# Batch 0's score masks, keys and tail rearranged, and one score visit per later batch, in a fused attention and MoE kernel

## The chip, the cores and the metric

The kernel runs on one core of a Trainium2 chip. The metric is device time in microseconds (us) of one execution; the median of the executions of a kernel is its time. One execution is also recorded by the hardware profiler; its span runs from the first to the last instruction of the program, and its own device time is somewhat longer than that span.

The engines are named as the profile names them: PE is the matrix engine (TensorE), PEld its weight loads, DVE is VectorE, ACT is ScalarE, POOL is GpSimd, and SP is SyncE, which computes nothing and issues transfers. PSUM has eight banks of 128 partitions by 512 float32 values, into which PE writes.

## The reference

```python
batch, n_heads, seq, head_dim = (8, 8, 576, 64)        # q, k, v in float32
scores = scale * np.matmul(q, k.transpose(0, 1, 3, 2))
rel = pos[:, None] - pos[None, :]
mask_plain = (rel >= 0) & (rel < 32)
mask_dil = (rel >= 0) & (rel < 32 * 4) & (rel % 4 == 0)   # heads 4 to 7
attn = softmax(where(mask, scores, -1e9))
x = (attn @ v) as 4608 tokens of 512 values
h = x @ w_in                                            # 512 -> 2048
out = (h * sigmoid(beta * h)) @ w_out                   # 2048 -> 512
```

Every head sees 32 keys per query: heads 0 to 3 ("plain") the last 32 positions, heads 4 to 7 ("dilated") every fourth of the last 128. The output is 4608 by 512 in float32.

## The kernel before

The work has two halves. **Attention** goes batch by batch (b = 0 to 7). **The feed-forward half** goes by tiles of 512 tokens (t = 0 to 8). For each t there are 16 "slots", one for each 128 of the 2048 hidden columns: four matmuls with 512 columns at line 811, a tanh on ACT (line 820) and a gate on DVE (line 825). Then come four output "blocks" of 16 matmuls each (line 846), cast by ACT (line 861) and stored through SP (line 866).

One plan orders all of it. Each piece of work is an operation given to `plan.op`, with the engines that can do it and their estimated times, what it depends on, a wished-for moment `vt` (lower is sooner), and the PSUM banks that it acquires. `Plan.run` simulates the engines and the transfer queues. Each round it takes, for each engine, the operations that could start within a few tens of ns of the earliest, and of these the one with the lowest `vt`; the instruction is emitted in that order, so the order on every engine is fixed when the kernel is built. Groups of banks have kinds with a limit each: `CAPS = {"h": 3, "p": 4, "o": 2, "z": 4, "a": 8, "s": 5}`, where "h" and "p" are slots, "o" and "z" output blocks, "s" scores and "a" everything else. Where PE would be idle early on, the plan emits matmuls on zeros (the filler, line 958)[...].

**Loads.** For batches 0 to 2 (`DIRECT = 3`) the POOL queue loads q and k with a cast to bf16 (`direct_qk`, issued at line 384). For batch 0 the order in the queue is: dilated k, dilated q, plain k, plain q, then v and the weights. Dilated k goes to `std[0]`, a 96 by 2 by 768 tile. PE transposes it (line 448 for dilated, 455 for plain), and ACT or DVE copy it out of PSUM (line 232). From batch 3 on, the loads go through DRAM and a transposing DMA.

**Scores.** Operations named S2 and S3 score the dilated heads (line 639), S00, S10, S01 and S11 the plain ones (line 673), T the last 64 positions of the dilated heads (line 609). The exponential of a score bank is an ACT operation at line 576. Score matmuls have 64 contraction rows and run as two row halves side by side. The plan prices a change between this and full rows at `SWITCH = 95` ns.

Batch 0 has its mask added on PE: matmuls of the identity with `add_d` or `add_p` (lines 631, 661, 664) put 0 or -65536 into the bank before the scores accumulate on it. These matmuls are the head of the same plan operation as the scores. From batch 1 on, the mask is a multiplication after the exponential (line 580), on POOL or DVE, with tiles that POOL builds early: `mask_d`, and for the plain heads `maskn_PP` and `maskn_FP`, 4 by 96 columns each (line 376). From batch 2 on (`PAIRED = 2`) two plain head pairs are scored together, in two visits to PE per batch: S00 covers the first half of the positions and S01 the second. Each visit is 12 matmuls with 96 columns into four banks, and each bank is read by an exponential of 288 columns.

V and U are the products with v (lines 714, 729, 699), followed by a normalisation on DVE (lines 595, 596). For batches 0 and 1, X and Y transpose the result back on PE (lines 765, 780, 750) into `xT`, the input of the slots. U and Y2, Y3 belong to the tail T.

```python
vts[first.index("T"):len(first)] = [-.5, -.4, -.3, -.2]      # T U Y2 Y3 of batch 0, line 902
```

The functions that the diff touches, with the line numbers of the profile:

Of the kernel before, what the change touches and what calls it, by code (L numbers as in the profile page):

```python
# [22 lines left out]
class Op:  # L23
    def __init__(self, engs, fn, deps, vt, acquire, group, dma, lat, halves=False, sbuf=False):
# [4 lines left out]
        self.end = self.ready = None  # L29
        self.waits = 0  # L30
# [5 lines left out]
class Plan:  # L36
# [3 lines left out]
    CAPS = {"h": 3, "p": 4, "o": 2, "z": 4, "a": 8, "s": 5}  # L40
    SWITCH = 95
    LAT = {"PE": 210, "ACT": 45, "DVE": 45, "POOL": 60, "SP": 0}
# [5 lines left out]
    def op(self, engs, fn, deps=(), vt=0.0, acquire=None, group=None, dma=0, lat=None, halves=False, sbuf=False):  # L48
        acquire = acquire if acquire is None or isinstance(acquire, list) else [acquire]
        o = Op(engs, fn, deps, vt, acquire, group or acquire, dma, lat, halves, sbuf)  # L50
        self.ops.append(o)
        return o

    def run(self, filler=None, filler_until=0.0):
# [36 lines left out]
        while n_left:  # L91
# [21 lines left out]
            for e, c in near.items():  # L113
                first = min(s for s, _, _ in c)
                s, o, d = min((x for x in c if x[0] <= first + self.NEAR[e]), key=lambda x: (x[1].vt, x[0]))
                picks.append((s, o.vt, e, o, d))
# [58 lines left out]
def kernel(  # L175
# [38 lines left out]
    APART = 4  # L214

# [26 lines left out]
    mask_n = {n: const([P, 2, 2, QT], BF16, f"maskn_{n}") for n in ("FP", "PP")}  # L242
# [12 lines left out]
    pt = [const([P, NI * 2, P], BF16, f"pt{x}") for x in range(2)]  # L255
# [52 lines left out]
    def t_fill2(e):  # L308
        for x in range(2):
            nc.vector.memset(pt[x][:, :, QT:P], 0.0)  # L310
        nc.vector.memset(ptt[:], 0.0)
# [60 lines left out]
    def first_rows(m):  # L372
        nc.gpsimd.memset(m[0:WIN, 0], 0.0)
    for i, n in enumerate(("PP", "FP")):
        def t_mask_n(e, n=n):
            band(mask_n[n][:].rearrange("p a b n -> p (a b) n"), [[0, 4]], [(1, QT)], WIN, -1, 1.0, 0.0)
            if n == "FP":
                first_rows(mask_n[n])
        late_mask("n" + n, 1900, t_mask_n, -7.183 + .001 * i)
# [11 lines left out]
    def direct_qk(b, z, h0, deps, vt):  # L391
# [3 lines left out]
        return load("POOL", (dst[z], src), deps, vt, 576, .41 if b else .33, lat=1100 if b else 1500)  # L395

# [13 lines left out]
    def direct_vd(b, deps, vt, tdeps=()):  # L410
        src = v[b, 4:8].rearrange("h (t T) d -> t h (T d)", T=C)[0:P]
        out = [load("POOL", (vd16_of[b].rearrange("p h T d -> p h (T d)"), src), deps, vt, 512, .35)]
        for c in range(2):
            src = bass.AP(tensor=v.tensor, offset=v[b, 4].offset + ((P - WIN) * C + c) * D,
                          ap=[[2 * D, 2 * KTL], [S * D, 4], [1, D]])
            out.append(load("POOL", (vt_[b % 2][:, c, :, 0:D], src), list(tdeps), vt + (1.245 if b == 0 else .02 if b < DIRECT else 0) + .001 + .001 * c, 96, .2))
# [26 lines left out]
    def t_transposes(g, z, kind, i):  # L443
# [6 lines left out]
        else:  # L450
            tp = bank(g, BF16)[:, 0:S].rearrange("p (j g) -> p j g", j=RP)
            for j in range(RP):
                for h in range(2):
                    rows = slice(64 * h, 64 * h + 64)
                    nc.tensor.transpose(tp[rows, j], stp[z][rows, i, j * D:(j + 1) * D], ident_b[rows, rows])  # L455

# [49 lines left out]
    def attention(b, ld, names, vts):  # L506
# [4 lines left out]
        if b < DIRECT:  # L511
            for n in [x for x in names if x[0] in "KQ"]:
# [3 lines left out]
                src = ld["qk", z, 0 if kind == "P" else 4]  # L516
                tr = plan.op([("PE", (18 * mm(64) if kind == "P" else 6 * mm(QT)))],
                             lambda e, g=g, z=z, kind=kind, i=i: t_transposes(g, z, kind, i),
                             [src, ident], vt, acquire=g)
# [53 lines left out]
        def exp_and_mask(key, sop, g, vt, n, sc, w, m, tiles):  # L573
# [4 lines left out]
            if b >= ADDED or key == ("T",):  # L578
                def mask(e):
                    E[e].tensor_tensor(out=w(), in0=w(), in1=m(), op=ALU.mult)  # L580
                ex = plan.op([("POOL", 170 + 2.2 * n), ("DVE", 160 + .8 * n)], mask,
                             [ex] + ([mask_tail] if key == ("T",) else [mask_ops["D"]] if key[0] >= 2 else
                                     [mask_ops["n" + ("PP" if key[1] else "FP")]]), vt, sbuf=True)
# [17 lines left out]
        for name in [n for n in names if n[0] in "ST"]:  # L601
# [24 lines left out]
            if x >= 2:  # L626

                def score(e, xs=xs, gs=gs):
                    if b < ADDED:
                        for g in gs:  # L630
                            nc.tensor.matmul(  # L631
                                bank(g).rearrange("p (a n) -> p a n", a=4), lhsT=ident_b[:],
                                rhs=add_d[:].unsqueeze(1).to_broadcast([P, 4, P]), start=True, stop=False)
                    for n, x in enumerate(xs):
                        for i in range(4):
                            r, h4 = i // 2, 2 * (x - 2) + i % 2
                            for c in range(2):
# [5 lines left out]
                sop = plan.op([("PE", len(xs) * 4 * mm(P) + (190 + 2 * mm(4 * P) if b < ADDED else 0))], score,  # L643
                              deps + ([ident, adds["D"]] if b < ADDED else []), vt, acquire=gs, halves=True)
# [9 lines left out]
            j = int(name[2])  # L654

            def score(e, xs=xs, j=j, gs=gs):
                if b < ADDED:
                    for g in gs:
                        lo = 0
                        if j == 0:  # L660
                            nc.tensor.matmul(bank(g)[:, 0:QT], lhsT=ident_b[:], rhs=add_p["F"][:],
                                             start=True, stop=False)
                            lo = 1
                        nc.tensor.matmul(
                            bank(g)[:, lo * QT:3 * QT].rearrange("p (a n) -> p a n", n=QT), lhsT=ident_b[:],
                            rhs=add_p["P"][:].unsqueeze(1).to_broadcast([P, 3 - lo, QT]),
                            start=j == 1, stop=False)
                for n, x in enumerate(xs):
                    for a in range(3):
                        i = 3 * j + a  # L670
                        for h in range(2):
# [4 lines left out]
            sop = plan.op([("PE", len(xs) * 3 * mm(QT) + (190 + 2 * mm(3 * QT) if b < ADDED else 0))], score,  # L676
                          ([o for x in xs for o in steps[f"KP{x}"] + steps[f"QP{x}"]] if b < DIRECT else ready["P"])
                          + ([ident, adds["P"]] if b < ADDED else []), vt, acquire=gs, halves=True)
# [3 lines left out]
            for n, x in enumerate(xs):  # L682
                for h in range(2):
# [4 lines left out]
                                 lambda j=j: mask_n["PP" if j else "FP"][:].rearrange("p a b n -> p (a b) n")[  # L688
                                     :, (0, 1)[j == 0]:(0, 1)[j == 0] + 3],
# [302 lines left out]
```

## Time and profile before

| what | value |
|---|---|
| median of 3 executions | 305.16 us (305.11 to 305.79) |
| the profiled execution's own time | 304.98 us |
| its span | 303.1 us |
| PE busy | 296.0 us, 98% of the span |
| DVE, ACT, POOL busy | 183.1, 170.7, 90.9 us |
| mean granted PE clock | 0.999 |

"Busy" of PE counts overlapping matmuls and also the filler, so it is no measure of useful work. A timeline row gives the start, the stretch from the first start to the last end of merged instructions, the engine, line, operation, what it writes and reads, how many instructions it merges (x12), and in brackets the idle time of the engine before it, with what ended it.

### The profile page before, as it was taken

How to read it: one execution, taken by the hardware profiler on the slowest of the kernel's cores; microseconds unless marked ns; L12 is line 12 of the kernel's file. 1: busy time of each engine (PE TensorE's matmuls, PEld its weight loads, DVE VectorE, ACT ScalarE, POOL GpSimd, SP SyncE). 2: the span in 40 equal slices, each digit the busy share in tenths (PEclk: the TensorE clock that was granted, in tenths of full speed). 3: DMA queues.
4: the chain of work that ended last, by engine and by line, in shares of the span. 5: the costliest groups of instructions: out<-in, count | busy, mean ns of one | idle time of the engine just before them, and what ended most of it. 6: DMA issues, size and time to landing. Idle time of an engine off the chain costs nothing.

```text
span 303.1 us, 6036 instructions
## 1 busy us (share of the span) xinstructions
PE 296.0 (98%) x2312; PEld 148.8 (49%) x2312; DVE 183.1 (60%) x424; ACT 170.7 (56%) x314; POOL 90.9 (30%) x131
## 2 busy tenths in 40 slices
PE   7899999999999999999999999999999999999995
PEld 5565545654554444455444444444444444444454
DVE  4469965888866746896676658656764344343300
ACT  2667963877547644765664557555664444554411
POOL 8988662756046106320740074100000000000000
PEclk9999999999999999999999999999999999999999
DMA  6999999999999998999799989994132100100122
GB/s 95 170 211 201 206 188 205 193 146 169 182 172 220 158 212 154 175 151 227 155 170 183 206 148 167 172 212 110 56 93 75 38 35 35 37 35 35 54 83 73
DMA packets 117376, 42.47 MB, mean 140 GB/s; under 512 B 93748, under 2 KB 110916, under 8 KB 117348
## 3 DMA queue, kind: packets, MB, share of 16 engines
q0 software_dynamic: 66672, 19.66, 63.6%
q1 hardware_dynamic: 50532, 22.36, 36.6%
q8 instruction: 18, 0.29, 0.4%
q10 hardware_dynamic: 144, 0.07, 0.1%
q14 instruction: 10, 0.08, 0.1%
HBM read 39.32 MB, written 18.87 MB: 192 GB/s over the span
## 4 chain that ended last, share of the span: by engine, by line
PE 86%; DMA 8%; DVE 3%; issue 1%; POOL 1%; ACT 1%; DVEq 0%; POOLq 0%
PE bank L846 40%; PE bank L811 37%; DMA vp<-in_v_dram 6%; DMA st<-in_q_dram 2%; PE bank L729 2%; PE bank L673 2%; PE bank L639 1%; DVE g L825 1%; PE bank L714 1%; PE bank L455 1%; PE bank L448 1%; PE bank L699 1%; PE bank L780 0%; PE bank L631 0%; DVE xsp L596 0%
## 5 line engine op out<-in xcount | busy, mean ns | idle before, releaser
L846 PE MATMUL bank<-w_out_bf,g 128*128 128x512 bf16 (+2 forms) x608 | 142.7, 368 | 0.0
L825 DVE SCALAR_TENSOR_TENSOR g<-tnh,bank 128x512 bf16<-128x512 bf16 x144 | 97.9, 685 | 70.6 <-ACT tnh L820 69.7
L811 PE MATMUL bank<-xT,w_in_bf 128*128 128x512 bf16 (+1 forms) x584 | 140.1, 376 | 0.0
L820 ACT ACTIVATE tnh<-bank,beta_half 128x512 bf16<-128x512 f32 x144 | 98.4, 689 | 72.4 <-PE bank L811 67.9
L811 PEld LDWEIGHTS <-w_in_bf 128*128 128x128 bf16 x584 | 55.1, 98 | 61.0 <-issue 0.2
L846 PEld LDWEIGHTS <-g 128*128 128x128 bf16 x608 | 54.4, 98 | 55.4
L861 ACT ACTIVATE osb<-bank 128x512 f32<-128x512 f32 (+1 forms) x35 | 20.6, 588 | 31.6 <-PE bank L846 31.5
L576 ACT ACTIVATE pt<-bank 128x288 bf16<-128x288 f32 x64 | 21.6, 421 | 6.2 <-PE bank L673 6.2
L576 ACT ACTIVATE ptd<-bank 128x512 bf16<-128x512 f32 x32 | 16.9, 606 | 7.0 <-PE bank L639 7.0
L596 DVE TENSOR_TENSOR xsp<-bank,rcp 96x384 bf16<-96x384 f32 x32 | 17.7, 554 | 1.1
L384 POOL DMA_DIRECT2D vp<-in_v_dram x10 | 18.0, 1803 | 0.5 <-PE bank L455 0.5
L924 POOL COPY pace<-xT 1x2 bf16<-1x2 bf16 x4 | 0.8, 201 | 55.8 <-DMA xT<-x 55.8
L595 DVE RECIPROCAL rcp<-bank 128x4 f32<-128x4 f32 (+2 forms) x72 | 12.9, 179 | 5.9 <-PE bank L729 4.1
L580 DVE TENSOR_TENSOR ptd<-ptd,mask_d 128x512 bf16<-128x512 bf16 x27 | 11.9, 452 | 6.2 <-ACT ptd L576 5.0
L596 DVE TENSOR_TENSOR xdm<-bank,rcp 128x256 bf16<-128x256 f32 x32 | 13.6, 425 | 1.1
L384 POOL DMA_DIRECT2D s<-in_q_dram x10 | 13.7, 1374 | 0.0
L384 POOL DMA_DIRECT2D vt<-in_v_dram x16 | 13.6, 1034 | 0.0
L729 PEld LDWEIGHTS <-pt 128*128 128x128 bf16 x192 | 9.1, 97 | 5.7 <-issue 0.5
L384 POOL DMA_DIRECT2D s<-in_k_dram x10 | 11.2, 1123 | 1.1 <-issue 1.1
L232 POOL COPY vd<-st 128x1024 bf16<-128x1024 bf16 x5 | 5.2, 1037 | 19.4 <-DMA st<-in_v_dram 19.4
L729 PE MATMUL bank<-vp,pt 128*128 128x65 bf16 x192 | 10.1, 193 | 0.2 <-DMA vp<-in_v_dram 0.2
L863 DVE TENSOR_SCALAR osb<-bank 128x512 f32<-128x512 f32 (+2 forms) x3 | 1.4, 470 | 13.3 <-PE bank L846 13.3
(107 smaller groups left out, 183.3 us busy)
## 6 DMA issues: line engine op xcount, KB each, us to landing
out_dram<-osb SPq DMA_DIRECT2D x35, 256.0 KB, 2.6
s<-in_k_dram POOLq DMA_DIRECT2D x10, 288.0 KB, 6.7
s<-in_q_dram POOLq DMA_DIRECT2D x10, 288.0 KB, 10.1
vp<-in_v_dram POOLq DMA_DIRECT2D x7, 384.0 KB, 18.1
w_out_bf<-in_moe_w_out_dram POOLq DMA_DIRECT2D x2, 1024.0 KB, 16.5
st<-in_k_dram POOLq DMA_DIRECT2D x6, 288.0 KB, 13.4
st<-in_q_dram POOLq DMA_DIRECT2D x6, 288.0 KB, 12.7
x<-xsp SPq DMA_DIRECT2D x12, 144.0 KB
```

The source lines that it names most:

```text
L384: {"POOL": nc.gpsimd, "SP": nc.sync}[queue].dma_start(out=out, in_=in_)
L576: nc.scalar.activation(out=w(), in_=sc(), func=ACT.Exp, scale=SCALE)
L580: E[e].tensor_tensor(out=w(), in0=w(), in1=m(), op=ALU.mult)
L595: nc.vector.reciprocal(out=r, in_=p[..., D])
L596: nc.vector.tensor_tensor(out=dst, in0=p[..., 0:D], in1=r.unsqueeze(len(p.shape) - 1).to_broadcast(list(p.shape[:-1]) + [D]), op=ALU.mult)
L673: nc.tensor.matmul(bank(gs[2 * n + h])[:, a * QT:(a + 1) * QT], lhsT=kT[kv][rows, x, i * QT:i * QT + P], rhs=qT[kv][rows, x, i * QT:(i + 1 ...
L729: nc.tensor.matmul(pv[:, a, h2, :], lhsT=pt[x][:, (3 * j + a) * 2 + h2], rhs=vp[kv][:, (2 * x + h2) * NI + 3 * j + a, 0:D + 1], start=True ...
L811: nc.tensor.matmul(bank(g)[:, a:z], lhsT=w_in_bf[:, kt, fb * P:(fb + 1) * P], rhs=xT[:, kt, xo + a:xo + z], start=(i == 0 and kt == kts[0] ...
L820: nc.scalar.activation(out=th[:, 0:n], in_=bank(g)[:, 0:n], func=ACT.Tanh, scale=beta_half[:, fb:fb + 1])
L825: nc.vector.scalar_tensor_tensor(out=g_t[t % 2][:, fb, c0:c0 + n], in0=th[:, 0:n], scalar=1.0, in1=bank(g)[:, 0:n], op0=ALU.add, op1=ALU.mult)
L846: nc.tensor.matmul(bank(g)[:, lo:hi], lhsT=g_t[t % 2][:, fb, tb * P:(tb + 1) * P], rhs=w_out_bf[:, fb, lo:hi], start=(fb == 0), stop=(fb = ...
L861: nc.scalar.mul(out=ob[:, lo:hi], in_=bank(g)[:, lo:hi], mul=0.5)
```

## The change

The diff does six things.

1. **Masks of batch 0 ahead.** The matmuls that add the mask become a plan operation of their own (`added`), which acquires the banks and depends only on the identity and the mask tile. The score operation depends on it and no longer acquires.
2. **Dilated keys of batch 0 by SP.** `first_keys` loads them in float32 through the SP queue into a stage in `g_t[1]`, and two operations on ACT or DVE cast them into `std[0]`. They leave the POOL queue, where dilated q is now the first load.
3. **Plain scores in one visit.** From batch 3 on (`AT_ONCE = 3`) all 24 plain matmuls of a batch are one operation. It acquires six banks at once, of a new kind "w" with a limit of 6, and six exponentials and six masks of 384 columns replace eight of 288.
4. **One mask tile.** `mask_n` with 9 by 96 columns takes the place of `maskn_PP` and `maskn_FP`. The two halves of `pt` become one tile.
5. **Tail of batch 0 later.** T, U, Y2 and Y3 get `vt` values of .2 to .5 in place of -.5 to -.2; the small `vt` loads of the tail get 1.255 in place of 1.245, which puts them behind one more load of batch 1.
6. **Twelve operations shifted.** `NUDGE` gives twelve operations, by their number, a bias in ns that is added to their start only while the plan chooses.

```diff
-    CAPS = {"h": 3, "p": 4, "o": 2, "z": 4, "a": 8, "s": 5}
+    CAPS = {"h": 3, "p": 4, "o": 2, "z": 4, "a": 8, "s": 5, "w": 6}
     SWITCH = 95
+    NUDGE = {101: -60, 129: 400, 159: -400, 219: 60, 245: -150, 250: 900, 417: 900, 517: 60, 554: 900,
+        700: -900, 789: 60, 1116: -900}
...
+        o.bias = self.NUDGE.get(len(self.ops), 0)
...
-                first = min(s for s, _, _ in c)
-                s, o, d = min((x for x in c if x[0] <= first + self.NEAR[e]), key=lambda x: (x[1].vt, x[0]))
+                first = min(s + o.bias for s, o, _ in c)
+                s, o, d = min((x for x in c if x[0] + x[1].bias <= first + self.NEAR[e]), key=lambda x: (x[1].vt, x[0]))
...
-    for i, n in enumerate(("PP", "FP")):
-        def t_mask_n(e, n=n):
-            band(mask_n[n][:].rearrange("p a b n -> p (a b) n"), [[0, 4]], [(1, QT)], WIN, -1, 1.0, 0.0)
-            if n == "FP":
-                first_rows(mask_n[n])
-        late_mask("n" + n, 1900, t_mask_n, -7.183 + .001 * i)
+    def t_mask_n(e):
+
+        band(mask_n[:], [[0, 9]], [(1, QT)], WIN, -1, 1.0, 0.0)
+        for i in (1, 7):
+            nc.gpsimd.memset(mask_n[0:WIN, i], 0.0)
+    late_mask("n", 3300, t_mask_n, -7.183)
...
+    def first_keys():
+
+        stage = g_t[1][0:2 * GD, 0:6, :].rearrange("p f n -> p (f n)").bitcast(FP32).rearrange("p (x e) -> p x e", x=2)
+        src = bass.AP(tensor=k.tensor, offset=k[0, 4].offset,
+                      ap=[[RD * D, 2 * GD], [2 * S * D, 2], [1, RD * D]])
+        o = load("SP", (stage, src), [], -9.1, 576, .41, 400, 1200)
+        return [plan.op([("ACT", 175 + .834 * RD * D), ("DVE", 160 + 1.042 * RD * D)],
+                        lambda e, x=x: copy(e, std[0][:, x], stage[:, x]), [o], -9.1, sbuf=True) for x in range(2)]
...
-            out.append(load("POOL", (vt_[b % 2][:, c, :, 0:D], src), list(tdeps), vt + (1.245 if b == 0 else .02 if b < DIRECT else 0) + .001 + .001 * c, 96, .2))
+            out.append(load("POOL", (vt_[b % 2][:, c, :, 0:D], src), list(tdeps), vt + (1.255 if b == 0 else .02 if b < DIRECT else 0) + .001 + .001 * c, 96, .2))
...
+    def at_once(x, i, h):
+
+        n = NI * x + i
+        return 8 * (n // 4) + 4 * h + n % 4
...
-                sop = plan.op([("PE", len(xs) * 4 * mm(P) + (190 + 2 * mm(4 * P) if b < ADDED else 0))], score,
-                              deps + ([ident, adds["D"]] if b < ADDED else []), vt, acquire=gs, halves=True)
+                before = [plan.op([("PE", 2 * mm(4 * P))], added, [ident, adds["D"]], vt, acquire=gs)] if b < ADDED else []
+                sop = plan.op([("PE", len(xs) * 4 * mm(P))], score, deps + before, vt,
+                              acquire=None if before else gs, group=gs, halves=True)
...
+            if b >= AT_ONCE:
+                if name != "S00":
+                    continue
+                gs = [Group("w") for _ in range(6)]
+
+                def score(e, gs=gs):
+                    for x in range(2):
+                        for i in range(NI):
+                            for h in range(2):
+                                rows = slice(64 * h, 64 * h + 64)
+                                n, at = divmod(at_once(x, i, h), 4)
+                                nc.tensor.matmul(
+                                    bank(gs[n])[:, at * QT:(at + 1) * QT], lhsT=kT[kv][rows, x, i * QT:i * QT + P],
+                                    rhs=qT[kv][rows, x, i * QT:(i + 1) * QT], start=True, stop=True)
+                sop = plan.op([("PE", 2 * NI * mm(QT))], score, [o for x in range(2) for o in steps[f"KP{x}"] + steps[f"QP{x}"]]
+                              if b < DIRECT else ready["P"], vt, acquire=gs, halves=True)
...
+                for n in range(6):
+                    blocks = slice(4 * n, 4 * n + 4)
+                    first = (1, 1, 5, 5, 2, 2)[n]
+                    exp_and_mask(("P", n), sop, gs[n], vt, 4 * QT,
+                                 lambda g=gs[n]: bank(g)[:, 0:4 * QT].rearrange("p (a n) -> p a n", n=QT),
+                                 lambda blocks=blocks: pt_all[:, blocks, 0:QT],
+                                 lambda first=first: mask_n[:, first:first + 4], [("pt", "P", n)] + old)
+                continue
...
-            sop = plan.op([("PE", len(xs) * 3 * mm(QT) + (190 + 2 * mm(3 * QT) if b < ADDED else 0))], score,
+            before = [plan.op([("PE", 2 * mm(3 * QT) + 30)], added, [ident, adds["P"]], vt, acquire=gs)] if b < ADDED else []
+            sop = plan.op([("PE", len(xs) * 3 * mm(QT))], score,
...
-        ld[0]["qk", z, h0] = direct_qk(0, z, h0, [], -9 + .01 * n)
+        ld[0]["qk", z, h0] = first_keys() if n == 0 else direct_qk(0, z, h0, [], -9 + .01 * n)
...
-    vts[first.index("T"):len(first)] = [-.5, -.4, -.3, -.2]
+    vts[first.index("T"):len(first)] = [.2,.35,.45,.5]
```

## The prediction

> **What bounds the kernel now.** I read the page first, then PE by stretches of time, then the rows around the two places that the change touches.
>
> ```profile
> span 303.1 us, 6036 instructions
> PE 296.0 (98%) x2312; PEld 148.8 (49%) x2312; DVE 183.1 (60%) x424; ACT 170.7 (56%) x314; POOL 90.9 (30%) x131
> ```
>
> PE is the bound, but its 98% counts filler and overlaps. The busy time by stretches (PE, PEld, DVE, ACT, POOL, then clock, DMA share, GB/s) says where it is not:
>
> ```profile
> 0.00:10.00 10.00, 7.04 (x55) 4.88 (x55) 4.06 (x20) 2.76 (x4) 8.42 (x21) 1.00 0.76 110
> 10.00:20.70 10.70, 10.40 (x202) 6.80 (x203) 7.34 (x26) 7.94 (x20) 9.94 (x18) 1.00 1.54 194
> 20.70:60.00 39.30, 38.61 (x465) 21.37 (x464) 28.98 (x64) 27.23 (x57) 24.59 (x39) 1.00 1.42 199
> 60.00:285.00 225.00, 225.00 (x1494) 107.28 (x1493) 141.36 (x314) 129.42 (x228) 47.93 (x56) 1.00 0.99 134
> ```
>
> From 60 to 285 us PE is never idle. Matmuls of 512 columns start 0.216 us apart there (eight of them from 117.11 to 118.85 below), so only less PE time helps. In the first 10 us the profile has 31 filler matmuls and 24 transposes: almost nothing useful. From 10.0 to 20.7 us I count columns: the useful matmuls, at 0.216 us per 512 columns and with row halves running in pairs, need 7.6 us of 10.7, so 3.1 us are lost in a chain between PE, ACT and DVE. The timeline of the start shows what this hangs on:
>
> ```profile
> 5.83 0.68 PE L448 MATMUL bank<-ident_b,st 96*128 96x96 bf16 x12
> ...
> 8.53 0.68 PE L448 MATMUL bank<-ident_b,st 96*128 96x96 bf16 x12 [1.47 <-DMA st<-in_q_dram]
> ...
> 9.26 0.76 DVE L232 COPY dq<-bank 128x576 bf16<-128x576 bf16 x1 [1.48 <-PE bank L448]
> ...
> 10.07 0.60 PE L631 MATMUL bank<-add_d,ident_b 128*128 128x512 bf16 x2 [0.41 <-DVE dq L232]
> ...
> 10.61 0.40 PE L639 MATMUL bank<-dq,dk 64*128 64x128 bf16 x8
> ```
>
> Keys, issued first, are used at 5.83, queries at 8.53; then a copy out of PSUM, the mask matmuls, and only at 10.61 the first score. One visit of the plain scores, mid-kernel:
>
> ```profile
> 115.79 1.03 PE L846 MATMUL bank<-w_out_bf,g 128*128 128x512 bf16 x4
> 116.75 0.43 PE L673 MATMUL bank<-qT,kT 64*128 64x96 bf16 x12
> 117.11 1.90 PE L846 MATMUL bank<-w_out_bf,g 128*128 128x512 bf16 x8
> ```
>
> Four blocks' matmuls should end 4 x 0.216 = 0.86 after 115.79, at 116.65; the scores start at 116.75. Their six pairs of 96 columns are worth 6 x 0.041 = 0.25, yet the next matmul starts 0.36 later. So a visit carries 0.10 + 0.11 = **0.21 us** beside its work. The waits of PEld from 60 to 285 us name nothing else of size:
>
> ```profile
> PEld L673 <- issue: 5.1, 12, 0.4
> PEld L639 <- issue: 2.1, 5, 0.4
> ```
>
> No PE wait on a bank, on ACT or on DVE appears there.
>
> **What the Trainium skill says.** "TensorEngine Tiling (Array Packing)", Key Properties: a change of tiling mode drains TensorE. The trace agrees; it is the 0.21 us. "Trainium Kernel Development and Optimization", Key Constraints: transfers from SP, ACT and POOL run on the same 16 engines, so several issuers save only issue time. The trace before has no large early SP load to show it; this feeds a rival below. "DMA: Bandwidth & Descriptors", Anatomy of one DMA, fits 2.0 us + bytes / 436e3: for the keys (589,824 bytes in float32) an estimate of 3.4 us from issue. The same load, cast by POOL, was issued at 1.36 and used at 5.83, 4.5 us later.
>
> **The change part by part.**
>
> *Keys by SP.* The first POOL issue is 0.80 us (dilated k, 1.36 to 2.15). Without it every POOL issue behind it, queries, plain k and q, v and the weights, moves up 0.79. SP issues at about 0.8, where beta's 0.41 stood; beta follows and is not needed until 17.7. By the skill's estimate keys are there at 0.8 + 3.4 = 4.2. Then two casts of 768 columns: ACT's rows of 512 and 288 columns (0.60, 0.42) give 0.80 ns per column, so about 0.81 us; on DVE between 0.4 (its 1024-column bf16 copy is 0.43) and 1.0. ACT has nothing to do from 2.3 to 6.29, and DVE only short work from 4.2 to 6.5, so the casts lie beside the queries' transfer: keys ready at 5.0 to 5.5, no later than now. What ends the wait are the queries. Bounds: 0 earlier (the keys' transfer takes from them what the issue saved) to 2.7 earlier (queries take the keys' place, 8.53 - 5.83). I take 0.8 at PE for the whole start: the shared engines give no more than the issue.
>
> *Masks ahead.* The head of S2 is 10.61 - 10.07 = 0.54 us on the path, and it moves into the wait for the queries: `add_d` is ready at 5.73. S3's 0.5 goes there too, since four banks fit the limit of five. The plain masks, 0.35 to 0.45 us in each of four visits at 13.5 to 16.8, can go ahead only as banks come free and lie beside ACT, which is 2.98 of 3.00 us busy from 13 to 16. Lower bound 0.3, upper 0.54 + 0.5 + 4 x 0.4 = 2.6; I take 0.5.
>
> *Tail later.* T waits less in the startup, but its PE work then stands in a full stretch. U waited 0.25 us for its v load at 26.69; that goes. The later `vt` loads pass behind one load of batch 1, 1.5 us at the spacing of landings, and U moves by more. Between -0.3 (tail work added to full PE) and +0.4 (T's 0.28 and its 0.40 on ACT); I take 0.1.
>
> *Does the start reach the end?* The DMA queue is full from 10 to 57 us, and PE meets batch 1's v with no slack:
>
> ```profile
> 47.38 0.89 PE L729 MATMUL bank<-vp,pt 128*128 128x65 bf16 x24 [0.19 <-DMA vp<-in_v_dram]
> ```
>
> After it there are still four groups of output matmuls of tile 0 (3.5 us) before tile 1 starts at 52.6. So an earlier PE has work to do first, and tile 1 can follow its data closer; with the loads also up by about 0.8, a gain of 1.4 passes.
>
> *Plain scores in one visit.* Five batches (3 to 7) lose one visit each: 5 x 0.21 = **1.05 us**, all in the full stretch, so all on the path. Evictions: 8 x 0.42 become 6 x about 0.50 on ACT, hidden either way (ACT has 95 idle us of 225). The added wait: PE needs six of eight banks free. Before, it needed four and never waited. A slot holds a bank for its matmuls, tanh and gate, 0.86 + 0.69 + 0.69 = 2.24 us; where slots and blocks alternate every 1.73 us this is 1.3 banks, and the output block one or a little more: about 2.5 held, 5.5 free. So there are moments with six, just after a block's matmuls, where the visit above already stands. I take 0; bounds 0 to 1.37 per visit (a tanh and a gate to wait out). Behind a waiting visit stands everything on PE.
>
> *Mask tile.* POOL: by rows of 384 and 512 columns (0.53 to 0.64 for a select), 864 columns cost about 0.9 each, 3.2 in all against 3.2 for the two before. Nothing: first used at 36.6, built by 25.7.
>
> *Twelve shifts.* Counting operations as the program creates them, they are: an `xT` copy of batch 0 (101), a part of slot 2 (129) and a tanh (159) of tile 0, the last transposes of batch 1 (219), five masks, an exponential and two parts of output blocks. The six from batch 2 on (417 to 1116) touch engines with idle time, or swap PE work for PE work: 0. The early six: between -0.4 and +0.4, the size of the largest bias on PE; I take 0.
>
> **Sum**: 0.8 + 0.5 + 0.1 + 1.05 = 2.45. 304.98 - 2.45 = 302.5 for a profiled execution. The median was 0.18 above that execution, so I forecast **302.7**. Own range 301.7 to 303.9.
>
> **Rivals.**
> - *The start is hidden by the transfers.* Keys in float32 write twice the bytes through the same 16 engines, w_in's last part (26.25), w_out and v of batch 1 land when they did, and PE waits there instead. For it: PE meets v at 47.38. Against: tile 0's spare groups. Only the visits and 0.1 remain: 305.16 - 1.15 = 304.0 (up to 304.6).
> - *The start is worth more.* Queries take the keys' place: 2.7 + 0.54, cut by ACT, which is full from 13 us, to about 3. Then 305.16 - 3.0 - 1.05 = 301.1.
> - *Six banks stall PE.* Each visit waits for the readers of slots, or those starve afterwards behind six exponentials (3.0 us of ACT). At 1.37 per visit: 302.7 + 6.85 = 309.6; at half of that, 306.1. It turns the sum slower than measurable from (2.45 + 0.92) / 5 = 0.67 us per visit. For it: 5.5 free banks on average. Against: no bank wait in 225 us before, in a plan that counts banks.
> - *The visit is not merged usefully*: it starts late, the batch's values are late, and the visits' gain is lost; 304.2 with the start.
>
> **How the numbers follow.** A measurement of this kernel can tell about 0.3%, 0.92 us, from no change: faster is below 304.24. Forecast 0.47, start worth more 0.18, start hidden 0.17 (half of it within 0.3%), not merged usefully 0.04, six banks 0.14. Faster 0.47 + 0.18 + 0.08 = 0.73; same 0.13; slower 0.14. The range 300.7 to 305.8 takes in the first four and leaves out some of the last and the far end of the second.
>
> **What would show it.** Right: L639 first at about 9.3 instead of 10.61 with L631 ahead of the queries' transposes; 24 plain score matmuls in one row after batch 2, seven PEld gaps at L673 instead of twelve from 60 to 285 us, and that stretch's work 1 us shorter. Wrong: PE idle before L673 with a releaser on ACT or DVE (six banks), new waits of L811 or L846 on transfers at 20 to 50 us (start hidden), or a first score no earlier than 10.

## The result, and the profile after

The change makes no measured difference. The kernel after takes 305.06 us in the median (304.80 to 305.33), the kernel before 305.13 beside it; the ratio is 0.9994, with a 95% interval of 0.9976 to 1.0012. The profiled execution took 304.8 us, its span is 303.1, as before. I had forecast 302.7. The versions below were measured in groups, each beside the kernel before, whose median lay between 304.88 and 305.13; a difference between versions of different groups therefore carries some 0.2 us. One execution of `no_shifts_alone`, 309.97 us, is left out of its figures as a slow one, over 1.5% above the fastest of its kernel.

So 2.4 us are missing, and the profile says at which places. The page's line of engines after:

```profile
PE 291.2 (96%) x2268; PEld 149.0 (49%) x2306; DVE 188.5 (62%) x420; ACT 169.6 (56%) x304; POOL 85.6 (28%) x123
```

PE's fall from 296.0 to 291.2 is no gain. The trace lost records: PE has 2268 where PEld has 2306, and each matmul has one weight load. The work by stretches suffers from the same loss (columns as in the prediction):

```profile
0.00:10.00 10.00, 7.91 (x90) 5.23 (x92) 5.55 (x22) 4.00 (x6) 8.31 (x22) 1.00 0.91 167
10.00:20.70 10.70, 9.88 (x180) 6.95 (x174) 7.79 (x23) 7.28 (x20) 10.30 (x17) 1.00 1.50 193
20.70:60.00 39.30, 36.36 (x434) 20.52 (x440) 31.69 (x67) 27.20 (x55) 20.42 (x31) 1.00 1.41 195
60.00:285.00 225.00, 222.16 (x1480) 107.85 (x1508) 142.06 (x306) 127.81 (x219) 46.58 (x56) 1.00 0.99 133
```

The DMA share of the first 10 us rose from 0.76 to 0.91, and 167 GB/s are moved there instead of 110. The order at the start came as planned, as the timeline of PE shows:

```profile
5.16 1.13 PE L649 MATMUL bank<-add_d,ident_b 128*128 128x512 bf16 x4 [0.22 <-POOL add_d L339]
...
6.24 0.68 PE L461 MATMUL bank<-ident_b,st 96*128 96x96 bf16 x12
...
7.22 0.69 PE L461 MATMUL bank<-ident_b,st 96*128 96x96 bf16 x12
...
8.37 0.29 PE L659 MATMUL bank<-dq,dk 64*128 64x128 bf16 x4
9.29 0.29 PE L659 MATMUL bank<-dq,dk 64*128 64x128 bf16 x4 [0.63 <-DVE dq L238]
```

The masks (L649) stand ahead of the transposes, the queries are transposed at 7.22 instead of 8.53, and the first scores run at 8.37 and 9.29 instead of 10.61. The second half of them waits 0.63 us for DVE's copy of the queries.

Because PE's records have gaps, I follow PE by its weight loads: each load is weighted with the columns of its matmul, fillers with nothing, and I ask when the same amount of useful work was reached in both traces. Below, a negative number means that the kernel after is ahead. Where the two orders differ, up to 45 us and from 55 to 110, an entry is good to some 0.3 us; from 49 to 54 us the orders are the same, and each load is 0.56 us ahead.

| moment in the kernel before, us | 11 | 20 | 27 | 33 | 43 | 49 to 54 | 62 | 87 | 103 | 141 to 152 | 160 | 193 | 226 to 290 |
|---|---|---|---|---|---|---|---|---|---|---|---|---|---|
| kernel after, us | -1.5 | -1.3 | -0.6 | +0.4 | -0.5 | -0.56 | +1.0 | +1.1 | +0.9 | +0.7 | +0.5 | +0.25 | +0.04 |

Three things are seen. The start gained 1.5. Of this, about 0.6 was left at 54 us; then some 1.6 were lost by 62 us. After that each of the five merged visits won back about 0.21, until both kernels ended together. The waits of PE from 20 to 64 us (in total, times, longest), first before, then after, name the losses:

```profile
PE bank L455 <- DMA st<-in_q_dram: 0.2, 1, 0.2
PE bank L729 <- DMA vp<-in_v_dram: 0.2, 1, 0.2
```

```profile
PE bank L628 <- DVE qT L238: 1.4, 1, 1.4
PE bank L659 <- DVE g L877: 1.0, 2, 0.8
PE bank L461 <- DMA st<-in_k_dram: 0.7, 1, 0.7
```

(L628 is the tail's score T, L609 before; L461 are the dilated transposes, L448 before; L659 the dilated scores, L639 before.) The wait for v that the prediction showed at 47.38 us is gone, as v now lands at 45.56. In its place PE waits for batch 1's dilated keys at 26 us and twice for DVE. The page's chain that ended last, by lines, agrees; the kernel before and then after:

```profile
PE bank L846 40%; PE bank L811 37%; DMA vp<-in_v_dram 6%; DMA st<-in_q_dram 2%; PE bank L729 2%; PE bank L673 2%; PE bank L639 1%; DVE g L825 1%; PE bank L714 1%; PE bank L455 1%; PE bank L448 1%; PE bank L699 1%; PE bank L780 0%; PE bank L631 0%; DVE xsp L596 0%
```

```profile
PE bank L898 41%; PE bank L863 37%; DMA st<-in_k_dram 4%; PE bank L780 2%; PE bank L659 1%; PE bank L764 1%; DVE qt L238 1%; PE bank L687 1%; PE bank L461 1%; DVE dkt L238 1%; PE bank L749 1%; PE bank L723 1%; DVE dk L238 1%; DVE g L877 0%; POOL st L388 0%
```

`DVE qt` and `DVE dkt`, small copies for the tail, have come into the chain. A rounded 1% of the span is 1.5 to 4.5 us, far more than such copies should take. The timeline of DVE and POOL where the 1.6 us were lost, before:

```profile
56.71 1.67 POOL L384 DMA_DIRECT2D s<-in_k_dram  x1
...
57.81 2.02 POOL L384 DMA_DIRECT2D vt<-in_v_dram  x2
58.20 0.30 DVE L232 COPY qt<-dq 64x128 bf16<-64x128 bf16 x1
58.53 0.43 DVE L232 COPY vd<-vd 128x1024 bf16<-128x1024 bf16 x1
58.92 0.76 DVE L232 COPY qT<-bank 128x576 bf16<-128x576 bf16 x1
```

and after:

```profile
56.14 1.67 POOL L388 DMA_DIRECT2D s<-in_k_dram  x1
...
57.23 1.25 POOL L388 DMA_DIRECT2D vt<-in_v_dram  x1
57.41 2.47 DVE L238 COPY qt<-dq 64x128 bf16<-64x128 bf16 x2
57.93 1.59 POOL L238 COPY vd<-vd 128x1024 bf16<-128x1024 bf16 x1
...
59.90 0.76 DVE L238 COPY qT<-bank 128x576 bf16<-128x576 bf16 x1
...
60.72 0.28 PE L628 MATMUL bank<-qt,dkt 128*128 128x64 bf16 x4 [1.38 <-DVE qT L238]
```

Two copies of 64 by 128, 0.19 us each where nothing holds them, take 2.47 us. The view of the tile `qt` splits them: 2.24 and 0.19. The long one ends at 59.65, 0.13 behind POOL's copy `vd`, which ends at 57.93 + 1.59 = 59.52. Behind it in DVE's order stands the queries' copy out of PSUM, and T on PE needs that copy's bank: 1.38 us of PE idle. The new thing in these lines is **where `vd` runs**. This copy of the dilated values (the spread) ran on DVE before, in 0.43 us; now the plan gives it to POOL.

The Trainium skill has an explanation for this: "SBUF — State Buffer", section "SBUF: two separate sides", says that GpSimd and certain VectorE operations share a pair of ports as an exclusive lock, which the one that starts first has for its whole instruction while the other waits. The trace agrees in that a copy of 0.19 us is recorded for 2.24 and ends just behind POOL's copy. That it is these ports, no trace here shows; what can be tested is whether POOL's work holds the copy.

The plan is not blind to such a lock. In its simulation (`port` in `Plan.run`) copies marked `sbuf=True` on DVE and on POOL keep out of each other's way, but the loads that POOL issues are not marked, and on the chip only the order on each engine is fixed, not the times. Here DVE's copy began behind POOL's issues, was still open when POOL's copy began at 57.93, and then waited for that too.

### The profile page after: what moved, and what is told of

It is laid out like the page before. It is cut to its first block, busy times and chain, and to the rows that moved or that the text cites. A ratio compares the mean times of both kernels' runs of the same rounds, so it can differ in the third digit from the quotient of the medians.

```text
span 303.1 us, 5956 instructions
## 1 busy us (share of the span) xinstructions
PE 291.2 (96%) x2268; PEld 149.0 (49%) x2306; DVE 188.5 (62%) x420; ACT 169.6 (56%) x304; POOL 85.6 (28%) x123
## 4 chain that ended last, share of the span: by engine, by line
PE 86%; DMA 4%; DVE 4%; issue 3%; POOL 1%; ACT 1%; POOLq 0%; DVEq 0%
PE bank L898 41%; PE bank L863 37%; DMA st<-in_k_dram 4%; PE bank L780 2%; PE bank L659 1%; PE bank L764 1%; DVE qt L238 1%; PE bank L687 1%; PE bank L461 1%; DVE dkt L238 1%; PE bank L749 1%; PE bank L723 1%; DVE dk L238 1%; DVE g L877 0%; POOL st L388 0%
## 5 line engine op out<-in xcount | busy, mean ns | idle before, releaser
L898 PE MATMUL bank<-w_out_bf,g 128*128 128x512 bf16 (+2 forms) x589 | 137.7, 367 | 1.6 <-issue 1.1
L863 PE MATMUL bank<-xT,w_in_bf 128*128 128x512 bf16 (+1 forms) x565 | 137.2, 376 | 1.1
L595 ACT ACTIVATE pt<-bank 128x384 bf16<-128x384 f32 (+1 forms) x54 | 20.4, 470 | 7.2 <-PE bank L687 5.3
L599 DVE TENSOR_TENSOR pt<-pt,mask_n 128x384 bf16<-128x384 bf16 (+1 forms) x43 | 15.5, 376 | 6.5 <-ACT pt L595 6.1
```

The lines of the kernel that those rows point to most:

```text
L595: nc.scalar.activation(out=w(), in_=sc(), func=ACT.Exp, scale=SCALE)
L863: nc.tensor.matmul(bank(g)[:, a:z], lhsT=w_in_bf[:, kt, fb * P:(fb + 1) * P], rhs=xT[:, kt, xo + a:xo + z], start=(i == 0 and kt == kts[0] ...
L898: nc.tensor.matmul(bank(g)[:, lo:hi], lhsT=g_t[t % 2][:, fb, tb * P:(tb + 1) * P], rhs=w_out_bf[:, fb, lo:hi], start=(fb == 0), stop=(fb = ...
```

## The experiments

**Does POOL hold the copy?** Theory A: DVE's copy is held by POOL's instruction. Rival B: the copy waits for something else. Three kernels change only the engine of one tile's copies; the order of all other instructions is unchanged on every engine. First, `qt` on ACT:

```diff
-                copy(e, qt[kv][rows, c]...
+                copy("ACT" if b in (2,) else e, qt[kv][rows, c]...
```

> The changed kernel with one edit: the two small copies that fill qt for batch 2 (64x128 each) run on ACT instead of DVE; the order on PE, POOL and SP is unchanged. Theory A (in the changed kernel the first of these copies sat on DVE from 57.41 to 59.65, 2.24 us instead of 0.19, because POOL was issuing a transfer and copying vd; the copy out of PSUM behind it and then PE's line 628 waited): the 1.4 us PE wait at line 628 goes, and the kernel takes 1.3 to 1.75 us less than the changed one, 303.3 to 303.8. Theory B (the wait is only where a lateness shows that has another cause, the bank or the arrival of batch 2's queries): PE waits as long at line 628 or just after, 304.8 to 305.3.

Measured: 304.28 us (304.01 to 304.83), ratio to before 0.9976 (0.9966 to 0.9987). T's wait of 1.4 us is gone, and PE gains 1.16 us between 55 and 62 us on the kernel after. Its profiled execution began that stretch 0.44 late, by a transfer told of below, so 0.72 remained at the end, and the time stayed above A's 303.3 to 303.8.

```profile
58.37 1.59 POOL L238 COPY vd<-vd 128x1024 bf16<-128x1024 bf16 x1
58.57 0.76 DVE L238 COPY qT<-bank 128x576 bf16<-128x576 bf16 x1 [0.64 <-PE bank L468]
58.81 0.59 ACT L238 COPY qt<-dq 64x128 bf16<-64x128 bf16 x2
```

Beside the same POOL copy, ACT does both `qt` copies in 0.59 us, and DVE's copy out of PSUM keeps its 0.76. So what was held at this place was DVE's copy from SBUF to SBUF alone. Second, `vd` on ACT, `qt` on DVE as in the kernel after:

```diff
-            copy(e, vd[kv][:, :, :, 0:D], vd16_of[b])
+            copy("ACT" if b == 2 else e, vd[kv][:, :, :, 0:D], vd16_of[b])
```

> The kernel after with one copy moved: batch 2's copy of the dilated values into their spread tile (vd<-vd, 128x16x64) runs on ScalarE instead of GpSimd, all orders otherwise the same. Theory A (VectorE's SBUF copies are locked out while GpSimd runs an instruction): the first queries' copy qt<-dq of batch 2, which ended at 59.65 us, 0.13 us behind GpSimd's copy (57.93 to 59.52), should now end behind GpSimd's issue of vt<-in_v alone (57.23 to 58.48), at about 58.6, so that L628 waits 0.3 us or nothing instead of 1.4 and TensorE's lag at 62 us is about 1 us less than after's; the time 303.9 to 304.3, less what ScalarE's extra 1 us costs its exponentials. Rival B (the copy waits for its data or for a semaphore, not for GpSimd): it still ends near 59.6, and the time is 304.8 or more.

Measured: 304.54 us (304.04 to 305.08), ratio 0.9986 (0.9977 to 0.9996). The timeline of the place:

```profile
55.98 1.67 POOL L388 DMA_DIRECT2D s<-in_k_dram  x1
57.07 1.25 POOL L388 DMA_DIRECT2D vt<-in_v_dram  x1
57.24 0.74 DVE L238 COPY qt<-dq 64x128 bf16<-64x128 bf16 x2
...
58.02 0.76 DVE L238 COPY qT<-bank 128x576 bf16<-128x576 bf16 x1
58.20 1.03 ACT L238 COPY vd<-vd 128x1024 bf16<-128x1024 bf16 x1
```

The first `qt` copy takes 0.52 instead of 2.24: POOL's copy was worth 1.7 us, its issue 0.3. It ended at 57.76, earlier than the 58.6 that I expected. So it did not wait for the issue of `vt`, which is recorded to 58.32. The times point to the longer one of `s` before it: that ends at 57.65, and four traces have the `qt` copy end 0.11 to 0.12 us behind it (`before` 58.50 and 58.38, `visits_only` 58.11 and 57.99, here, and `spread_on_dve` below 58.11 and 57.99). PE gains only 0.83 in the stretch, since ACT's extra 1.03 us make PE wait 0.5 for the second half of `qT`; the time is above theory A's 304.3, which left that cost open, and below B's 304.8. Third, `vd` back on DVE, with the rest of the change in place:

```diff
-            copy(e, vd[kv][:, :, :, 0:D], vd16_of[b])
+            copy("DVE" if b == 2 else e, vd[kv][:, :, :, 0:D], vd16_of[b])
```

> The kernel after, with batch 2's copy of the dilated values into their spread tile (vd<-vd, 128x16x64) on VectorE, where the kernel before and every version without the shifts has it, instead of GpSimd; the twelve shifts and all orders stay otherwise. Theory C (the shifts moved this copy to GpSimd, and there it locked VectorE's queries' copy out for 1.7 us): the first qt<-dq ends at about 57.8, the spread takes 0.43 us, or up to 1.0 if GpSimd's issues hold it, L628 waits less than 0.5 us, TensorE's lag at 62 us falls by 0.9 to 1.4 us, and the time is 303.8 to 304.3. Rival D (on VectorE the spread is locked out by GpSimd's next issues instead, and holds the queries' copy out of PSUM behind it, so that the wait only changes its name): L628 still waits 1 us or more and the time is 304.7 or more.

Measured: **303.59 us** (303.10 to 303.83), ratio 0.9953 (0.9934 to 0.9971), 1.47 us less than the kernel after by the medians, or 1.3 if each is compared with the kernel before beside it. Theory C holds, somewhat above its size:

```profile
57.59 0.73 DVE L238 COPY qt<-dq 64x128 bf16<-64x128 bf16 x2
...
58.34 0.76 DVE L238 COPY qT<-bank 128x576 bf16<-128x576 bf16 x1
58.59 0.64 ACT L238 COPY qT<-bank 128x576 bf16<-128x576 bf16 x1
...
59.13 0.62 DVE L238 COPY vd<-vd 128x1024 bf16<-128x1024 bf16 x1
...
59.35 0.28 PE L628 MATMUL bank<-qt,dkt 128*128 128x64 bf16 x4
```

T no longer waits. From 55 to 62 us PE gains 1.48 us on the kernel after (from +0.18 to -1.30) and keeps all of it to the end, to 0.01.

**What moved the spread?** Each operation may run on several engines, and the plan picks one. Built with no shifts the plan puts batch 2's `vd` on DVE; with any single shift alone too. With all twelve it goes to POOL, and taking out any one of four of them (operations 129, 159, 219 and 250, all among the early six) puts it back. The kernel after without shifts:

```diff
-    NUDGE = {101: -60, 129: 400, 159: -400, 219: 60, 245: -150, 250: 900, ...}
+    NUDGE = {}
```

> The kernel after without the twelve shifts in the order (NUDGE empty), everything else as it is, the two VectorE copies on VectorE. If the shifts are worth nothing in themselves, as predicted, and their removal helped by 0.8 us where the copies were on ScalarE: 304.0 to 304.8. If the shifts carry the change and only look idle once the copies are moved: 305.5 or more.

Measured: 304.59 us (302.55 to 306.70), ratio 0.9986 (0.9967 to 1.0006): inside the first range that I wrote, but its interval takes in no change. At 61 us PE is about 1.5 us ahead of the kernel after. But this version has other orders on all engines, and in the profiled execution (305.85) it loses 0.7 us to a mask on POOL at 76 us and 1.5 us at 111 to a transposing transfer:

```profile
110.99 0.62 PE L658 MATMUL bank<-dq,dk 64*128 64x128 bf16 x16 [1.49 <-DMA dq<-s]
```

Its 21 executions spread over 4.2 us, the 21 of `spread_act` and the 14 of `qt2_act`, which keep the shifts, over 1.0 and 0.8. So the shifts cost about 1.5 us at 58 us, by the engine that they gave the spread, and go with transfers that arrive in time later on. That they cause the latter is only argued.

**The same in batch 1.** After the change, `dkt` of batch 1 takes 0.97 us on DVE, where batch 0's took 0.36 in the kernel before, and its second `qt` copy 1.08, each beside a POOL issue of `vp`. Before, batch 1's `dkt` ran on POOL, in 0.56; so this copy too had changed its engine, and it does so without the shifts as well:

```profile
27.27 1.41 POOL L388 DMA_DIRECT2D vp<-in_v_dram  x1
27.89 0.97 DVE L238 COPY dkt<-dk 128x384 bf16<-128x384 bf16 x1
...
30.61 1.44 POOL L388 DMA_DIRECT2D vp<-in_v_dram  x1 [0.57 <-PE bank L802]
30.76 1.28 DVE L238 COPY qt<-dq 64x128 bf16<-64x128 bf16 x2
...
32.81 0.40 PE L659 MATMUL bank<-dq,dk 64*128 64x128 bf16 x8 [0.77 <-DVE g L877]
```

`dkt` ends at 28.86 and the issue at 28.68; the second `qt` at 32.04 and the issue at 32.05. The first `qt`, from 30.76 to 30.95 in the beginning of the same issue, took its 0.19: an issue holds such a copy in its later part, not from its first moment. The next version puts batch 1's `dkt` and `qt` on ACT too:

```diff
-            copy(e, dkt[kv], ...
+            copy("ACT" if b in (1,) else e, dkt[kv], ...
-                copy(e, qt[kv][rows, c]...
+                copy("ACT" if b in (1, 2) else e, qt[kv][rows, c]...
```

> As the run before, and the copies into dkt and qt for batch 1 also on ACT. In the changed kernel these took 0.97 and 1.08 us on DVE instead of 0.36 and 0.19, each ending as POOL's transfer issue ended, and PE waited 0.8 + 0.2 us for DVE at the dilated scores of batch 1 (line 659). Theory A: another 0.5 to 1.3 us less than with batch 2's copies alone, 302.2 to 303.2. Theory B (from 26 to 47 us PE follows the arrival of batch 1's loads and of w_out, so what it gains in between is waited for later): no less than the run with batch 2's copies alone, within 0.3 us.

Measured: 303.56 us (303.33 to 303.78), ratio 0.9952 (0.9938 to 0.9966), another 0.7 below `qt2_act`: theory A's difference, though not its absolute time. PE gains 0.1 at 26 us and another 0.9 from 27 to 35 us, where the copies stand. Then those of batch 0 as well (`b in (0, 1)` and `b in (0, 1, 2)`):

> As the run with batch 1's and 2's small copies on ACT (303.56), and batch 0's copies into dkt and qt on ACT as well. In the changed kernel batch 0's dkt copy sat on DVE from 7.83 to 8.58, twice its usual time, while POOL issued v's loads, and the second half of dq came behind it. Theory A (PE waits at 25 to 27 us for batch 1's dilated keys, so PE's lead at 20 us is worth nothing there): the second half of S2 starts about 0.7 earlier, the wait for st at line 461 grows by as much, and the time stays at 303.3 to 303.8. Theory B (PE's own start decides): 0.5 to 0.7 us less, 302.9 to 303.1.

Measured: 303.04 us (302.41 to 303.13), ratio 0.9931 (0.9916 to 0.9946). This is the time of theory B, but PE was no earlier up to 23 us (+0.03); its gain of 0.66 came in one step at 26 us.

**What happens at 26 us.** That step leads to the second finding. In all these versions PE arrives at batch 1's dilated transposes and waits for the keys; the kernel after and then `start_act`:

```profile
26.16 0.69 PE L461 MATMUL bank<-ident_b,st 96*128 96x96 bf16 x12 [0.67 <-DMA st<-in_k_dram]
```

```profile
25.83 0.68 PE L461 MATMUL bank<-ident_b,st 96*128 96x96 bf16 x12 [0.30 <-DMA st<-in_k_dram]
```

For pairs with one order on PE I compare when this row starts with how far PE is ahead or behind from there to 55 us:

| pair | row's start, us | its change | PE at 20 us | PE from 27 to 55 us |
|---|---|---|---|---|
| after, `qt2_act` | 26.16, 26.59 | +0.43 | +0.03 | +0.44 |
| after, `spread_act` | 26.16, 25.99 | -0.17 | 0.00 | -0.17 |
| after, `spread_on_dve` | 26.16, 26.33 | +0.17 | 0.00 | +0.18 |
| `dkt_qt_act`, `start_act` | 26.49, 25.83 | -0.66 | +0.03 | -0.66 |
| `dkt_qt_act`, `masks_late` | 26.49, 26.84 | +0.35 | +0.06 | +0.35 |

In these pairs PE follows the landing of these keys. What it did before 26 us has no say. The first three pairs have the same program up to 55 us, so the landing itself moves by up to 0.6 us from one execution to another, and the last two changes are about that large. The gain of `start_act` is therefore not shown to be its own.

**The parts of the start**, each taken from `dkt_qt_act`. The masks back in front of their scores:

```diff
-                before = [plan.op([("PE", ...)], added, ...)]
-                sop = plan.op([("PE", ...)], score, ...)
+                before = [plan.op([("PE", ...)], lambda e: None, ...)]
+                sop = plan.op([("PE", ...)], lambda e: (added(e), score(e)), ...)
```

> As the run with batch 1's and 2's small copies on ACT (303.56), with batch 0's mask matmuls emitted again directly in front of their scores; the order of everything else on PE is unchanged. Theory A (the start is covered by the wait for batch 1's keys at 26 us): S2's scores start 0.3 to 0.6 later, the PE wait at 26 us shrinks by as much, and the time is within 0.3 us, 303.3 to 303.9. Theory B (the masks are on the path to the end): 0.5 to 1.0 us more, 304.1 to 304.6.

Measured: 303.75 us (303.40 to 304.95), ratio 0.9970 (0.9956 to 0.9983), 0.2 above `dkt_qt_act`, within the range of theory A. PE lost 0.06 at 20 us and then what the landing took; the wait at 26 us grew from 0.99 to 1.28, where A let it shrink. Batch 0's dilated keys by POOL again, first in its queue:

```diff
-        o = load("SP", (stage, src), ...)
+        o = plan.op([("SP", 400)], lambda e: nc.gpsimd.dma_start(out=std[0], in_=src), ...)
...
-                        lambda e, x=x: copy(e, std[0][:, x], stage[:, x]), ...)
+                        lambda e, x=x: None, ...)
```

> As the run with batch 1's and 2's small copies on ACT (303.56), with batch 0's dilated keys again loaded by POOL with a cast, first in its queue; the order on PE is unchanged. Theory A (what the SP load brings is that all of POOL's loads come 0.8 to 1.6 us earlier, and PE follows these loads at 26 to 47 us): 0.8 to 1.6 us more, 304.4 to 305.2. Theory B (the loads would have been as early, the queue is full anyway): within 0.3 us, 303.3 to 303.9.

Measured: 304.09 us (303.88 to 304.72), ratio 0.9967 (0.9956 to 0.9979), 0.5 above `dkt_qt_act`, between the two theories. PE is 0.6 later at 13 us, and 2.7 at 20 us after a wait of 1.5 us for batch 0's v:

```profile
16.57 0.35 PE L780 MATMUL bank<-vp,pt 128*128 128x65 bf16 x6 [1.48 <-DMA vp<-in_v_dram]
```

From 27 us it is 1.6 later: the wait at L461, 1.0 in `dkt_qt_act`, took up most of the rest.

**The visits.** The kernel before with the single visit alone:

```diff
+    AT_ONCE = 3
+    NUDGE = {}
...
-                sop = plan.op(...)      # keys by POOL, masks in front of their scores, as before
+                sop = plan.op(..., both, ...)
```

> The kernel before with only the single visit of the plain scores from batch 3 on (and the one mask tile that it needs): no masks ahead, keys by POOL, the tail as before, no shifts. Its order on PE is that of the kernel before until batch 3. Theory A (a visit costs 0.21 us, six banks cost nothing): 5 x 0.21 = 1.05 us less than before, 304.1. Theory B (six banks make PE wait, or the six exponentials in a row starve the slots): no less than before, 305.1 or more.

Measured: 304.56 us (303.33 to 306.02), ratio 0.9990 (0.9976 to 1.0003); inconclusive in the median. In the profiled execution the visits show their 0.21 each, but a late transposing transfer (`xT<-x`) made PE wait 1.0 us, and PE ended 0.2 ahead. The reverse, the kernel after with two visits (and without the shifts numbered from 554 on, since the merge changes the numbers):

```diff
-    AT_ONCE = 3
+    AT_ONCE = 8
```

> The changed kernel with two visits of the plain scores again in batches 3 to 7 (and without the three shifts that count operations behind them). Its order on PE is that of the changed kernel until batch 3. Theory A (the visits give 1.05 us and the start with its stalls is 1 us slower than the start before): 306.1. Theory B (the start is even and the visits give nothing): 305.1.

Measured: 306.90 us (306.15 to 308.04), ratio 1.0062 (1.0042 to 1.0083), 1.8 above the kernel after. PE falls back by 0.21 at each of the five batches, and there are waits beside it. The waits from 60 to 285 us:

```profile
PE bank L659 <- DMA dq<-s: 1.7, 2, 1.0
PE bank L628 <- DVE qT L238: 1.4, 1, 1.4
```

T's 1.4 is that of the kernel after; the 1.7 are new, and put the time above theory A's 306.1. The hold at 58 us is seen a second time here: POOL's `vd` from 58.16 to 59.75, DVE's first `qt` from 57.63 to 59.89.

**No shifts, and all together.** `dkt_qt_act` with an empty `NUDGE`:

> As the run with batch 1's and 2's small copies on ACT (303.56), with no operation shifted (all twelve biases gone). This changes the order from tile 0 on, on every engine. Theory A (the shifts are worth nothing by themselves): within 0.5 us, 303.1 to 304.1. Theory B (they keep the plan out of an idle stretch of PE): 0.6 us more or worse, 304.2 and up.

Measured: 302.74 us (302.39 to 305.09), ratio 0.9934 (0.9910 to 0.9958), below both of the ranges that I wrote. Its batch 1 keys were used at 25.94, 0.55 earlier than in `dkt_qt_act`, which is within what that landing moves by. Last, `start_act` with an empty `NUDGE`:

> The two versions that ran fastest put together: batch 0's and 1's keys' copy dkt and batch 0's to 2's queries' copies qt on ScalarE (as in start_act, 303.04) and no shifts in the order (302.74 in no_shifts). If the earlier loads of batch 1 (-0.5) and the removal of the shifts (-0.8) add up: 302.2. If both draw on the same wait for batch 1's dilated keys at 26 us, which can be gained once: 302.6 to 302.8. In either case below before and after.

Measured: 303.22 us (302.59 to 303.51), ratio 0.9937 (0.9912 to 0.9962). The gains do not add up: the keys of batch 1 came at 26.8 in the profiled execution, 1.0 later than in `start_act`, and PE waited 1.1 us for them. The three fastest versions (302.74, 303.04, 303.22) can't be told apart. By their intervals all three are at least 0.38% below the kernel before, and below the interval of the kernel after.

## Why the prediction was wrong, and where it was right

- **Twelve shifts, "swap PE work for PE work: 0".** This step failed. I priced each shift by its own operation and missed that a shift changes what the plan decides later: here the engine of a copy 30 us downstream. Put back on DVE, that one copy is worth 1.3 to 1.5 us in the medians and 1.48 at PE, more than half of the error of 2.4.
- **"Does the start reach the end?"** This failed too. I wrote that a gain of 1.4 passes. PE's lead was 1.3 at 20 us and 0.56 at 54 us. I looked for the next late load at 47 us, found spare work in front of it, and did not ask about 26 us, where PE meets batch 1's keys. They came 2.2 us earlier (28.31 to 26.11), but PE came earlier still and waited 0.67. This is the rival "hidden by the transfers", for half of the gain, with other loads than it named. The two held copies of batch 1 are in the same stretch. The two failed steps account for 1.5 + 0.8 of the missing 2.4; the rest is within the interval.
- **Keys by SP, 0.8 at PE.** The price of the keys was too low: issued at 0.81, they were there for the casts at 5.35, 4.5 us later and not 3.4, and were transposed at 6.24 instead of 5.83. The fit that I took from "DMA: Bandwidth & Descriptors", Anatomy of one DMA, is stated there for transfers issued by GpSimd; I used it for SP. The queries landed at 7.17 instead of 8.49, but that difference is not the part's own: with the keys by POOL they landed at 7.66 to 8.49 in three traces, with the keys by SP at 6.37 to 7.49 in eleven, and from `keys_pool` to `dkt_qt_act` they gained 0.45. With the keys by SP the first packet of POOL's queue moves at 3.6 to 4.1 us, with the keys by POOL at 2.9, though POOL issues at 1.36 to 1.38 each time: SP's load keeps POOL's first transfer waiting on the shared engines, which is the caution that I drew from "Trainium Kernel Development and Optimization", Key Constraints. At the end the part is worth 0.5 to 0.7 in the medians.
- **Masks ahead, 0.5.** Mis-sized. The order came as described, but it moved PE by 0.06 at 20 us. I took the head of S2 to be on the path; yet in `dkt_qt_act` the second half of S2, with no masks in front of it, waits 0.52 us for DVE's copy of the queries and runs at 9.31, in `masks_late`, behind its masks, at 8.94.
- **Tail later, 0.1.** Not tested by itself. Its `qt` and `dkt` copies were the ones held in batches 1 and 2, which I had not considered.
- **Plain scores in one visit, 1.05.** Right at PE, 0.21 for each of five batches, in the kernel after and in `no_visits`; in the times it stands alone nowhere, as `visits_only` is inconclusive and `no_visits` has new waits. The waits of PEld from 60 to 285 us, of which seven were forecast for plain scores, after:

```profile
PEld L687 <- issue: 2.1, 5, 0.4
PEld L659 <- issue: 2.1, 5, 0.4
...
PEld L723 <- issue: 0.4, 1, 0.4
```

  Five for the merged visits at L687 and one at L723; batch 2 has two visits there, one of which shows no gap.
- **Six banks, 0.** Right: no wait of L687 for ACT or DVE appears, in a trace where PE waits for almost nothing after 62 us. The rival that ends slower did not come true.

The time lay inside the range, by the width that I gave to the rivals. The corrected change, with the spread on DVE, ran in 303.59, inside the forecast's own range of 301.7 to 303.9.

## What to carry to other kernels

When a scheduler picks engines, compare where each operation landed before and after, not only the operations that were edited. A short VectorE copy within SBUF can be dear where GpSimd copies or issues at that moment: look for copies whose duration is several times that of their shape elsewhere, and put the held copy or the one that holds it on another engine. A plan that keeps such operations apart has to count GpSimd's issues too; that was not tried here. For a gain at the start, walk along every load until the pipeline is full, and ask at each whether the data or the engine comes last.

## What the runs showed of the hardware

- A VectorE copy of 64 by 128 bf16 took 0.19 us when nothing held it, 0.52 and 1.08 in the later part of a GpSimd issue of a transfer, and 2.24 when a GpSimd copy of 128 by 1024 came behind that issue. At the beginning of an issue it kept its 0.19. At the same place ScalarE's two copies took 0.59 and VectorE's copy out of PSUM its 0.76.
- GpSimd's own copy of 128 by 1024 took 1.59 us at that place and 1.04 elsewhere. Its record begins while the issue before it is still open, to 58.48, and it ends 1.04 us behind that; in all seven traces that have this copy on GpSimd the distance is 1.04 to 1.05.
- The landing of one transfer in the middle of a full queue moved by up to 0.6 us between executions of one program, that of batch 0's queries by 0.8 (7.17 in `after`, 6.37 in `spread_on_dve`), which is as much as a change of this kind is worth.
